# Attention and two feed-forward layers on one core: the values' products in float32, with each head's values among zeros

## The chip, the cores and the metric

The kernel runs on one core of a Trainium2 chip. The metric is the device time in microseconds, from the first instruction to the last, of one execution of the whole program. Three timed runs of the kernel before are given, and one execution with the hardware profiler, from which every row below is taken. The engines are called by the profile's short names: PE (TensorE's matrix products), PEld (its loads of the stationary operand), DVE (VectorE), ACT (ScalarE), POOL (GpSimd) and SP (SyncE, which here does nothing but issue DMAs).

## The reference, cut to what matters

Attention over 4 batches, 8 heads, 576 positions and a head size of 64, where each query sees itself and the 127 positions before it, with a penalty that grows with the distance; then a gated feed-forward layer of 1536 columns and a second one of 2048 columns over the 2304 rows that result. The weights come as float64.

```python
scores = scale * np.matmul(q, k.transpose(0, 1, 3, 2))
scores = np.where(mask, scores + bias[None], -1000000000.0)
attn = np.exp(scores - np.max(scores, axis=-1, keepdims=True))
attn = attn / (np.sum(attn, axis=-1, keepdims=True) + 1e-09)
x = np.matmul(attn, v)              # then heads side by side: 2304 x 512
x = (x @ w_a) * (x @ w_b) @ w_out   # 1536 columns between
h = x @ w_in
g = np.where(h >= 1, h, np.where(h <= -1, 0, (h + 1) ** 2 / 4))
out = g @ w_out2                    # 2048 columns between
```

## The kernel before, in words

**Two number formats on PE.** A float32 operand can be used as it is, and then the profile shows two matrix instructions and two weight loads for each product the program names (the scores of line 314 are named 144 times and stand in the profile 288 times). Or it is cut into a high and a low part of the type float32r, and three products are added: high by high, high by low, low by high. All feed-forward products do the latter (lines 576 to 578, 649, 677 to 679, 709 to 711); the parts are made by a copy that rounds (`ecopy`, or `nc.scalar.copy`) and a subtraction (`minus`, line 149).

**Attention** is cut into units: a batch, one of two parts of its positions (part 0 is positions 0 to 255, part 1 is 256 to 575), and a pair of heads. There are 32 units, taken batch by batch. A unit has rounds `m`, each for two blocks of 64 queries: `m` 0 and 1 in part 0, `m` 2, 3 and 4 in part 1, the last with one block alone. So there are 80 rounds, 20 in each batch. The two heads of a pair stand together in the 128 partitions: queries of head 0 in partitions 0 to 63, of head 1 in 64 to 127.

A round goes through three functions. `scores` (line 304) multiplies queries and keys (line 314), lets DVE add the penalty and find the maximum (line 320), ACT take the exponential with its sum (line 324), DVE add 1e-9 to the sum and invert it (lines 329 and 330), and then scales the first block's probabilities on POOL (line 338) and the second block's on ACT (line 334). `transposes` (line 343) turns the probabilities, three blocks of 128 columns in a full round, with a product by the identity matrix, and copies them from PSUM. `values` (line 396) multiplies them by the values, and every second round the sums go into the input of the feed-forward layer, high part by ACT and low part by DVE (lines 449 and 450), once for each head.

Values and probabilities are treated in two ways before. In batch 0 (the set `WHOLE`) they stay float32: a full round multiplies two whole blocks of 128 keys (lines 411 and 414), the first half of a block (64 rows, line 411) and a block `odd` whose first 64 rows are zero. In batches 1 to 3 they are cut in parts: POOL cuts the values (lines 292 and 293), ACT and DVE the turned probabilities (lines 389 and 391), which lie in tiles with zero quarters, and a full round is six float32r products of 256 columns (line 430), the round `m` = 0 three. The last round `m` = 4 is float32 everywhere, with a product of 128 rows and one of 64 (lines 407 and 408).

**Order of the work.** `attention` (line 461) is a generator of steps; for round `n` it emits the scores of `n`, the transposes of `n` - 3 and the values of `n` - 5. When a new unit begins it prepares the next unit (`prep_unit`) and issues the loads of the one after that (`load_unit`, `AHEAD` = 2). Between the products of the feed-forward layer the main loop takes steps of attention at a hand-set pace (`PACE`, 0.8 steps to a product group at first, then 0.5), and where products need rows that are not there (`ready`), it takes steps alone. The decoding of the float64 weights is emitted between them too (`pump`, `decode`): for the first 15 blocks two of its operations are POOL's (line 541 and the subtraction of line 543), the other five or six are DVE's. A scheduler then orders each engine's instructions by this order and by its own estimate of when each is ready; on the chip every engine takes its instructions strictly in that order. All DMAs are issued by SP, in one queue.

The first loads are `load_start` (line 201): queries, keys and values of batch 0, part 0, into tiles of the weights' pool (`wp`), whose first three slots they hold.

Of the kernel before, what the change touches and what calls it, by code (L numbers as in the profile page):

```python
# [26 lines left out]
def attention_and_two_ffns(  # L27
# [41 lines left out]
    E_V = ['PP', 'PP', 'PP', 'PP', 'PP', 'PP', 'PP', 'PP']  # L69
    E_VO = 'A'  # L70
    E_X = ['A', 'A', 'A', 'A', 'A', 'A', 'A', 'A']
    E_Y = 'AV'
    E_Z = 'P'
# [8 lines left out]
    NWHOLE = 2  # L82
# [3 lines left out]
    PW = 2  # L86
# [5 lines left out]
    VP = 2  # L92
    VT = 3
# [5 lines left out]
    WHOLE = {(0, p) for p in range(NWHOLE)}  # L99
# [26 lines left out]
    rel = att.tile([P, 2, 3 * D], F32, tag="s_sb", name="rel", bufs=SB)[:, 0]  # L126
# [57 lines left out]
    turned = []  # L184
    for z in range(PT):
        pair = tuple(
            att.tile([P, 4, P], F32R, tag=f"p{w}{z}", name=f"p{w}{z}", bufs=1) for w in "hl"
        )
        for t in pair:
            for me, at, other in ((slice(D), 1, slice(D, P)), (slice(D, P), 2, slice(D))):  # L190
                ecopy(
                    E_Z, t[me, at].rearrange("p (n t) -> p n t", t=D), diag[0][me, :2, other]
                )
        turned.append(pair)
# [6 lines left out]
    def load_start():  # L201
        for nm in "qkv":
            start[nm] = [
                wp.tile([P, H, D], F32, tag=f"w{z}", name=f"{nm}{z}") for z in "hl"
            ]
        src = {"q": q, "k": k, "v": v}
        for nm, h0, h1, hi_ in LORD:
            for t, t0 in zip(start[nm], (0, P)):
# [11 lines left out]
    def value_parts():  # L220
        return [att.tile([P, NV - 1, P], F32R, tag=f"v{z}", name=f"v{z}", bufs=VP) for z in "hl"]

    def turn_start(hp):
# [7 lines left out]
        for j in range(2):  # L231
# [3 lines left out]
        prep[0, 0, hp] = (  # L235
            qd, kt,
            [t[:, 2 * hp : 2 * hp + 2, :].rearrange("p h d -> p (h d)") for t in start["v"]],
            start["odd"][:, 2 * hp : 2 * hp + 2, :].rearrange("p h d -> p (h d)"),
        )

    def load_unit(b, part, hp):
# [15 lines left out]
        vt = att.tile([P, NV, 2, D], F32, tag="vt", name="vt", bufs=VT)  # L257
        n = (q1 - k0) // P
        for j in range(2):
            nc.sync.dma_start(  # L260
                vt[:, :n, j, :],
                v[b, 2 * hp + j, k0 : k0 + n * P, :].rearrange("(n p) d -> p n d", p=P),
            )
        if q1 == S:
            nc.sync.dma_start(
                vt[:D, n, :, :],
                v[b, 2 * hp : 2 * hp + 2, S - D :, :].rearrange("j p d -> p j d"),
            )
        prep[b, part, hp] = (t["q"], t["k"], vt)

    def prep_unit(u):
# [5 lines left out]
        qr, kr, vt = prep[b, part, hp]  # L277
# [8 lines left out]
        vt = vt.rearrange("p n j d -> p n (j d)")  # L286
        if (b, part) in WHOLE:
            prep[b, part, hp] = (qd, kt, vt, None)
            return
# [4 lines left out]
        prep[b, part, hp] = (qd, kt, vt, vs)  # L294
# [7 lines left out]
    rounds = {}  # L302

    def scores(b, hp, m):
        part = int(m >= 2)
        q0, _, k0 = PART[part]
        qd, kt = prep[b, part, hp][:2]
        ps = ps_at.tile([P, 2, 4 * D], F32, tag="at", name="ps_s")
        s_sb = att.tile([P, 2, 3 * D], F32, tag="s_sb", name="s_sb", bufs=SB)
# [8 lines left out]
        for z, i in enumerate(qblocks(m)):  # L318
            cs = slice(first_col(i), 3 * D)
            nc.vector.tensor_tensor_reduce(  # L320
                s_sb[:, z, cs], ps[:, z, cs], biases[hp][:, cs], -QSCALE, BIG,
# [3 lines left out]
                s_sb[:, z, cs], s_sb[:, z, cs], AF.Exp,  # L325
# [3 lines left out]
        nc.vector.tensor_scalar(ssum[:, :n], ssum[:, :n], 1e-9, None, ALU.add)  # L329
        nc.vector.reciprocal(ssum[:, :n], ssum[:, :n])  # L330
        for z, i in enumerate(qblocks(m)):
            cs = slice(first_col(i), 3 * D)
            if E_N[2 * b + part][z] == "A":
                nc.scalar.activation(
                    s_sb[:, z, cs], s_sb[:, z, cs], AF.Copy, scale=ssum[:, z : z + 1]
                )
                continue
            ENG[E_N[2 * b + part][z]].tensor_scalar(  # L338
                s_sb[:, z, cs], s_sb[:, z, cs], ssum[:, z : z + 1], None, ALU.mult
# [3 lines left out]
    def transposes(b, hp, m):  # L343


        s_sb = rounds.pop((b, hp, m)).rearrange("p z k -> p (z k)")
        ps = ps_at.tile([P, 4, P], F32, tag="at", name="ps_t")
        part = int(m >= 2)
        if (b, part) in WHOLE and m < ROUNDS - 1:
            if part and m == 2:  # L350
                vt = prep[b, part, hp][2]
                odd = start["odd"].rearrange("p (u n j) d -> p u n (j d)", u=2, n=2)[:, hp % 2]
                ecopy(E_VO, odd[D:], vt[D:, :2])
                prep[b, part, hp] = prep[b, part, hp][:3] + (odd,)
            pt = att.tile([P, 3, P], F32, tag="pt", name="pt", bufs=PW)
            for z in range(m == 0, 3):
                n = D if (m, z) == (0, 1) else P
                nc.tensor.transpose(ps[:n, z, :], s_sb[:, z * P : z * P + n], ident)
            if m == 0:
                ecopy(E_T[2 * b + (m >= 2)][0], pt[:D, 1], ps[:D, 1])  # L360
                ecopy(E_T[2 * b + (m >= 2)][1], pt[:, 2], ps[:, 2])
            else:
                ecopy(E_T[2 * b + (m >= 2)][0], pt, ps[:, :3])
            rounds[b, hp, m] = pt
            return
        if m == ROUNDS - 1:
            pt = att.tile([P, 3, P], F32, tag="pt", name="pt", bufs=PW)
            nc.tensor.transpose(ps[:, 0, :], s_sb[:, :P], ident)
            nc.tensor.transpose(ps[:D, 1, :], s_sb[:, P : P + D], ident)
            ecopy(E_T[2 * b + (m >= 2)][0], pt[:, 0], ps[:, 0])  # L370
            ecopy(E_T[2 * b + (m >= 2)][1], pt[:D, 1], ps[:D, 1])
            rounds[b, hp, m] = pt
            return
        count["t"] += 1
        ph, pl = turned[count["t"] % PT]
        if m == 0:
            nc.tensor.transpose(ps[:D, 1, :], s_sb[:, P : P + D], ident)
            nc.tensor.transpose(ps[:, 3, :], s_sb[:, 2 * P :], ident)
            cuts = [(slice(P), slice(3, 4), slice(3, 4)), (slice(D), slice(2, 3), slice(1, 2))]
        else:  # L380
            for z, at in enumerate((0, 1, 3)):
                nc.tensor.transpose(ps[:, at, :], s_sb[:, z * P : (z + 1) * P], ident)  # L382
            cuts = [
                (slice(P), slice(0, 4, 3), slice(0, 4, 3)),
                (slice(D), slice(2, 3), slice(1, 2)),
                (slice(D, P), slice(1, 2), slice(1, 2)),
            ]
        for n, (me, to, at) in enumerate(cuts):
            ecopy(E_T[2 * b + (m >= 2)][n > 0], ph[me, to], ps[me, at])
# [441 lines left out]
```

## Time and profile before

| | us |
|---|---|
| median of three runs | 1018.1 |
| the three runs | 1021.05, 1016.41, 1018.1 |
| the profiled execution's own time | 1016.69 |
| its span in the profile | 1014.9 |
| PE busy | 989.9 |
| DVE busy | 681.5 |
| ACT busy | 444.4 |
| POOL busy | 222.6 |

The span runs from the first to the last instruction that the profiler recorded; the execution's own time is 1.8 us longer. Busy times are unions of instruction spans. PE's instructions overlap in a pipeline and their ends are modelled, so PE can be busy without a break and still take its instructions at more than one pace: the distance from one start to the next tells more than the duration. An idle stretch in front of an instruction is put down to what ended it.

### The profile page before, as it was taken

Reading aid. Unit: us, or ns where it says so; the run is one execution under the profiler, and the core shown is the slowest. Engines: PE = TensorE matmul, PEld = TensorE weight load, DVE = VectorE, ACT = ScalarE, POOL = GpSimd, SP = SyncE. Lnnn points to the kernel's source line nnn. Section 1 sums busy time; section 2 is a strip of 40 time slices with the busy share of each in tenths; the row PEclk is TensorE's granted clock in tenths of the full one; section 3 lists DMA queues with packets and bytes.
Section 4 is the critical chain, followed back from the end, with each engine's and each line's share of the span. In section 5 each row is a group of like instructions: output and inputs, shape, how many; then the busy total and the mean of one; then the engine's idle time right before and its main releaser. Section 6 shows DMA issues by size and latency. Waiting matters only on the chain.

```text
span 1014.9 us, 15950 instructions
## 1 busy us (share of the span) xinstructions
PE 989.9 (98%) x5608; PEld 868.7 (86%) x5608; DVE 681.5 (67%) x1678; ACT 444.4 (44%) x1156; POOL 222.6 (22%) x268
## 2 busy tenths in 40 slices
PE   5899999999999999999999999999999999999998
PEld 4789899999999988888988888888888888888887
DVE  7998967868747899212898279833996446744443
ACT  5876677777644343111343234433552223322222
POOL 6685853544411100000122223000020000000001
PEclk9998999999999999999999999999999999999999
DMA  8756334335043443000223002200231000001111
GB/s 177 138 124 139 87 67 91 66 70 101 11 181 111 146 165 106 1 1 1 63 86 102 1 23 82 83 1 0 63 104 42 1 1 21 1 1 42 42 42 63
DMA packets 136512, 67.10 MB, mean 66 GB/s; under 512 B 107120, under 2 KB 127600, under 8 KB 135920
## 3 DMA queue, kind: packets, MB, share of 16 engines
q1 hardware_dynamic: 136432, 66.09, 24.4%
q8 instruction: 44, 0.72, 0.3%
q14 instruction: 36, 0.29, 0.1%
HBM read 56.62 MB, written 9.44 MB: 65 GB/s over the span
## 4 chain that ended last, share of the span: by engine, by line
PE 84%; DVE 3%; issue 1%; DMA 0%; ACT 0%; DVEq 0%; SPq 0%; ACTq 0%
PE mm L576 15%; PE mm L577 15%; PE mm L578 15%; PE acc L710 6%; PE acc L709 6%; PE acc L711 6%; PE acc L649 5%; PE acc L679 3%; PE acc L677 3%; PE acc L678 3%; PE ps_o L430 3%; PE ps_s L314 3%; PE ps_t L382 1%; PE ps_o L408 0%; DVE e L535 0%
## 5 line engine op out<-in xcount | busy, mean ns | idle before, releaser
L576 PE MATMUL mm<-xh,wh 128*128 128x512 f32 (+1 forms) x952 | 323.0, 340 | 1.9 <-DVE c_sb L633 0.8
L577 PE MATMUL mm<-xl,wh 128*128 128x512 f32 (+1 forms) x952 | 322.6, 339 | 0.8 <-DVE xl L149 0.8
L578 PE MATMUL mm<-xh,wl 128*128 128x512 f32 (+1 forms) x952 | 322.7, 339 | 0.0
L576 PEld LDWEIGHTS mm<-xh,wh 128*128 128x128 f32 x952 | 179.7, 189 | 22.9 <-DVE c_sb L633 1.2
L577 PEld LDWEIGHTS mm<-xl,wh 128*128 128x128 f32 x952 | 180.2, 189 | 20.8 <-DVE xl L149 1.1
L578 PEld LDWEIGHTS mm<-xh,wl 128*128 128x128 f32 x952 | 180.1, 189 | 19.4
L632 ACT ACTIVATE c_sb<-c_sb,half 128x512 f32<-128x512 f32 (+1 forms) x80 | 54.6, 682 | 166.6 <-DVE c_sb L631 166.6
L709 PE MATMUL acc<-wh,gh 128*128 128x512 f32 x288 | 112.3, 390 | 0.0
L710 PE MATMUL acc<-wl,gh 128*128 128x512 f32 x288 | 112.2, 390 | 0.0
L711 PE MATMUL acc<-wh,gl 128*128 128x512 f32 x288 | 110.4, 390 | 0.0
L631 DVE TENSOR_SCALAR c_sb<-mm 128x512 f32<-128x512 f32 (+1 forms) x80 | 50.8, 636 | 82.0 <-PE mm L578 79.2
L149 POOL TENSOR_TENSOR gl<-c_sb,gh 128x256 fp32r<-128x256 f32 x16 | 14.2, 891 | 386.3 <-ACT gh L598 379.2
L621 DVE TENSOR_TENSOR a_sb<-mm,a_sb 128x256 f32<-128x256 f32 (+1 forms) x79 | 40.7, 516 | 85.3 <-PE mm L578 77.3
L149 POOL TENSOR_TENSOR gl<-a_sb,gh 128x256 fp32r<-128x256 f32 x50 | 41.3, 827 | 236.2 <-ACT gh L598 236.2
L633 DVE SCALAR_TENSOR_TENSOR c_sb<-mm,c_sb 128x512 f32<-128x512 f32 (+1 forms) x80 | 50.7, 635 | 39.1 <-ACT c_sb L632 39.0
L338 POOL TENSOR_SCALAR s_sb<-s_sb,ssum 128x192 f32<-128x192 f32 (+1 forms) x80 | 62.5, 782 | 63.0 <-DVE ssum L330 39.0
L324 ACT ACTIVATE s_sb<-s_sb,nmax 128x192 f32<-128x192 f32 (+2 forms) x144 | 62.3, 434 | 25.7 <-DVE nmax L320 24.6
L598 ACT CAST gh<-c_sb 128x512 fp32r<-128x512 f32 (+1 forms) x80 | 46.3, 579 | 56.2 <-DVE c_sb L633 47.4
L598 ACT CAST gh<-a_sb 128x256 fp32r<-128x256 f32 (+1 forms) x79 | 38.2, 484 | 69.2 <-DVE a_sb L621 68.7
L525 ACT ACTIVATE e<-w 128x512 f32<-128x512 f32 x65 | 43.7, 673 | 56.6 <-DMA w<-in_moe_w_out_dram 11.8
L542 ACT CAST wh<-e 128x512 fp32r<-128x512 f32 x68 | 42.3, 621 | 59.3 <-DVE e L541 38.4
L149 DVE TENSOR_TENSOR gl<-c_sb,gh 128x512 fp32r<-128x512 f32 x64 | 44.2, 690 | 32.7 <-ACT gh L598 32.4
(112 smaller groups left out, 1891.4 us busy)
## 6 DMA issues: line engine op xcount, KB each, us to landing
w<-in_moe_w_out_dram SPq DMA_DIRECT2D x28, 512.0 KB, 3.5
w<-in_moe_w_in_dram SPq DMA_DIRECT2D x16, 512.0 KB, 3.6
w<-in_moe_w_a_dram SPq DMA_DIRECT2D x12, 512.0 KB, 4.3
w<-in_moe_w_b_dram SPq DMA_DIRECT2D x12, 512.0 KB, 4.5
x2p<-y SPq DMA_DIRECT2D x18, 256.0 KB, 2.2
out_dram<-osum SPq DMA_DIRECT2D x18, 256.0 KB, 2.0
xsum<-x2p SPq DMA_DIRECT2D x4, 1024.0 KB, 5.9
kraw<-in_k_dram SPq DMA_DIRECT2D x64, 56.0 KB, 2.7
```

Source lines behind the costliest of these rows:

```text
L149: eng.tensor_tensor(out_, a, hi.bitcast(F32), ALU.subtract)
L324: nc.scalar.activation(s_sb[:, z, cs], s_sb[:, z, cs], AF.Exp, bias=nmax[:, z : z + 1], scale=-1.0, accum_out=ssum[:, z : z + 1],)
L338: ENG[E_N[2 * b + part][z]].tensor_scalar(s_sb[:, z, cs], s_sb[:, z, cs], ssum[:, z : z + 1], None, ALU.mult)
L576: nc.tensor.matmul(ps, wh[:, cs], xh[:, c], start=(c == 0), stop=False)
L577: nc.tensor.matmul(ps, wh[:, cs], xl[:, c], start=False, stop=False)
L578: nc.tensor.matmul(ps, wl[:, cs], xh[:, c], start=False, stop=(c == NC - 1))
L598: nc.scalar.copy(hi[:, :n], t[:, :n])
L631: nc.vector.tensor_scalar(c_sb[:, :n], ph[:, :n], -1.0, None, ALU.max)
L632: nc.scalar.activation(c_sb[:, :n], c_sb[:, :n], AF.Square, bias=half, scale=0.5)
L709: nc.tensor.matmul(accs[s], gh[:, ss], wh, start=begin, stop=False)
L710: nc.tensor.matmul(accs[s], gh[:, ss], wl, start=False, stop=False)
L711: nc.tensor.matmul(accs[s], gl[:, ss], wh, start=False, stop=end)
```

## The change

The hi and lo parts of values and probabilities are gone in all batches, and so are `odd` and the products of 64 rows. Values are loaded into four standing tiles `vpad` of 4 blocks x 2 heads x 128 columns, where head 0's values fill columns 0 to 63 and head 1's columns 64 to 127, and POOL writes zeros into the other halves once. Probabilities are written into four standing tiles `padded` of 2 query blocks x 256 columns, the second block shifted by 64, with zeros around them. A round turns four blocks of 128 columns (two for `m` = 0 and `m` = 4) and copies them from PSUM at once. `values` multiplies, for each of two key blocks and each head, a 128 x 128 block of values among zeros by 128 columns of probabilities (64 in `m` = 4), in float32, all into the same 128 columns of PSUM; so both heads' sums lie under each other in the partitions, and go to the feed-forward input for both heads at once, after the last round of a part. The sum's 1e-9 is added on POOL and not on DVE, and POOL's scaling has a second factor of 1. Values are loaded when their unit begins and not two units ahead, each head's last 64 rows by a DMA of its own. The values of the start take four slots of `wp` in place of three for queries, keys and values, and eight DMAs in place of two.

```diff
-    turned = []
-    for z in range(PT):
...
+    padded = []
+    for z in range(SB):
+        t = att.tile([P, 2, 4 * D], F32, tag=f"s{z}", name=f"s{z}", bufs=1)
+        nc.gpsimd.memset(t[:, 0, 3 * D :], 0.0)
+        nc.gpsimd.memset(t[:, 1, :D], 0.0)
+        padded.append(t)
+    def clear_others(t):
+        for j in range(2):
+            nc.gpsimd.memset(t[:, :, j, (1 - j) * D : (2 - j) * D], 0.0)
+    vpad = []
+    for z in range(VT):
+        t = att.tile([P, NV, 2, P], F32, tag=f"v{z}", name=f"v{z}", bufs=1)
+        clear_others(t)
+        if TAIL < P:
+            nc.gpsimd.memset(t[TAIL:, NV - 1], 0.0)
...
+                for hp in range(NPAIR):
+                    for j in range(2):
+                        nc.sync.dma_start(
+                            start["v"][hp][:, :, j, j * D : (j + 1) * D],
+                            v[0, 2 * hp + j, : 2 * P, :].rearrange("(n p) d -> p n d", p=P),
+                        )
...
-        for _ in range(3):
+        for _ in range(4):
             slots[0][2].append(None)
-        odd = start["odd"] = att.tile([P, H, D], F32, tag="odd", name="odd", bufs=1)
-        nc.vector.memset(odd[:D], 0.0)
-        ecopy(E_VO, odd[D:], start["v"][0][D:])
...
+    def load_values(b, part, hp):
+        if b == 0 and part == 0:
+            return start["v"][hp]
...
+        vt = vpad[z]
         n = (q1 - k0) // P
         for j in range(2):
             nc.sync.dma_start(
-                vt[:, :n, j, :],
+                vt[:, :n, j, j * D : (j + 1) * D],
...
+            for j in range(2):
+                nc.sync.dma_start(
+                    vt[:TAIL, n, j, j * D : (j + 1) * D], v[b, 2 * hp + j, S - TAIL :, :]
+                )
...
-        vs = value_parts()
-        n = (q1 - k0) // P
-        ecopy(E_V[2 * b + part][0], vs[0][:, :n], vt[:, :n])
-        minus(ENG[E_V[2 * b + part][1]], vs[1][:, :n], vt[:, :n], vs[0][:, :n])
...
-        nc.vector.tensor_scalar(ssum[:, :n], ssum[:, :n], 1e-9, None, ALU.add)
+        nc.gpsimd.tensor_scalar(ssum[:, :n], ssum[:, :n], 1e-9, 1.0, ALU.add, ALU.mult)
         nc.vector.reciprocal(ssum[:, :n], ssum[:, :n])
...
+        for u in range(us.start, 2):
+            for z in range(n):
+                nc.tensor.transpose(ps[:, 2 * u + z, :], s_sb[:, z, u * P : (u + 1) * P], ident)
+        pt = att.tile([P, 2, 2, P], F32, tag="pt", name="pt", bufs=PT)
+        ecopy(
+            E_T[2 * b + part][0], pt[:, us, :n], ps.rearrange("p (u z) t -> p u z t", z=2)[:, us, :n]
+        )
...
+        opens, closes = m in (0, 2), m in (1, ROUNDS - 1)
...
+        todo_ = [(u, j) for u in range(m == 0, 2) for j in range(2)]
+        for e, (u, j) in enumerate(todo_):
+            nc.tensor.matmul(
+                dst, vt[:, m - 1 + u - k0 // P, j, :], pt[:, u, :n, j * D : (j + 1) * D],
+                start=opens and e == 0, stop=e == len(todo_) - 1, skip_group_check=True,
+            )
...
-            for j in range(2):
-                me = slice(j * D, (j + 1) * D)
...
-                ecopy(E_X[2 * b + part], xh, src)
-                minus(nc.vector, xl, src, xh)
+            xh, xl = (x[:, hp, t - t0 : t - t0 + w] for x in xs[i])
+            ecopy(E_X[2 * b + part], xh, po[:, at : at + w])
+            minus(nc.vector, xl, po[:, at : at + w], xh)
...
+                    values_of[units[u]] = load_values(*units[u])
```

## Rows read from the trace of the kernel before

**Rows 1.** The page's head and its busy times by engine.

```profile
span 1014.9 us, 15950 instructions
PE 989.9 (98%) x5608; PEld 868.7 (86%) x5608; DVE 681.5 (67%) x1678; ACT 444.4 (44%) x1156; POOL 222.6 (22%) x268
```

**Rows 2.** Busy time by stretch, with instructions; then granted clock, DMA share, GB/s.

```profile
0.00:33.00 33.00, 19.80 (x96) 15.99 (x97) 27.30 (x98) 20.23 (x67) 19.93 (x37) 0.95 0.82 172
33.00:85.00 52.00, 46.74 (x299) 40.57 (x298) 47.06 (x157) 39.54 (x129) 38.36 (x38) 0.93 0.58 127
100.00:125.00 25.00, 23.56 (x182) 22.39 (x181) 24.46 (x77) 16.97 (x57) 20.66 (x21) 1.00 0.44 100
150.00:200.00 50.00, 50.00 (x403) 49.23 (x401) 40.79 (x173) 37.91 (x143) 23.17 (x35) 1.00 0.40 77
```

**Rows 3.** Who waited for whom before 85 us, DVE's waits, the two longest.

```profile
DVE e L527 <- DMA w<-in_moe_w_a_dram: 3.2, 1, 3.2
DVE s_sb L320 <- PE ps_s L314: 3.0, 2, 2.7
```

**Rows 4.** PE's timeline near 204 us: start, duration, line, shape, count.

```profile
204.13 0.81 PE L314 MATMUL ps_s<-kt,diag 128*128 128x192 f32 x4
204.78 0.49 PE L382 MATMUL ps_t<-ident,s_sb 128*128 128x128 f32 x3
...
205.22 0.29 PE L430 MATMUL ps_o<-pl,vh 128*128 128x256 f32 x1
205.34 0.28 PE L430 MATMUL ps_o<-ph,vl 128*128 128x256 f32 x1
```

**Rows 5.** PE's timeline: a round `m` = 0 from 91.66, its scores.

```profile
91.66 0.61 PE L314 MATMUL ps_s<-kt,diag 128*128 128x64 f32 x4
...
92.22 0.28 PE L576 MATMUL mm<-xh,wh 128*128 128x256 f32 x1
```

**Rows 6.** PE's timeline: values of a last round, and of full rounds of batch 0.

```profile
141.26 0.38 PE L407 MATMUL ps_o<-pt,vt 128*128 128x128 f32 x2
...
142.21 0.28 PE L649 MATMUL acc<-gh,wl 128*128 128x256 f32 x1
...
45.78 1.13 PE L416 MATMUL ps_o<-pt,vt 64*128 64x128 f32 x6 [0.63 <-ACT pt L155]
...
47.06 1.13 PE L416 MATMUL ps_o<-pt,vt 64*128 64x128 f32 x6
```

**Rows 7.** Groups of instructions with shapes: count, busy us, mean ns, idle before.

```profile
L149 DVE TENSOR_TENSOR xl<-ps_o,xh 64x256 fp32r<-64x256 f32 x40 | 16.8, 419 | 3.2 <-ACT xh L155 2.2
L329 DVE TENSOR_SCALAR ssum<-ssum 128x2 f32<-128x2 f32 x64 | 14.4, 227 | 4.7 <-ACT s_sb L324 4.4
L338 POOL TENSOR_SCALAR s_sb<-s_sb,ssum 128x192 f32<-128x192 f32 x64 | 53.6, 839 | 51.3 <-DVE ssum L330 30.2 <-PE ps_s L314 5.8 <-ACT xh L155 4.3
L338 POOL TENSOR_SCALAR s_sb<-s_sb,ssum 128x64 f32<-128x64 f32 x16 | 8.9, 555 | 11.7 <-DVE ssum L330 8.8 <-PE ps_o L416 1.3 <-DMA w<-in_moe_w_b_dram 1.0
masks.py:197 POOL MEMSET ident<- 128x128 f32 x1 | 0.2, 206 | 0.3 <-POOLq L815 0.3
```

**Rows 8.** DVE's and POOL's timelines: one DVE line beside two kinds of POOL work.

```profile
32.38 1.30 DVE L528 TENSOR_SCALAR e<-e 128x512 f32<-128x512 f32 x1
32.13 1.27 POOL L541 TENSOR_TENSOR e<-up,e 128x512 f32<-128x512 f32 x1 [1.98 <-DVE ssum L330]
40.86 0.43 DVE L528 TENSOR_SCALAR e<-e 128x512 f32<-128x512 f32 x1
40.82 1.02 POOL L338 TENSOR_SCALAR s_sb<-s_sb,ssum 128x192 f32<-128x192 f32 x1 [0.99 <-DVE ssum L330]
```

**Rows 9.** SP's queue: a load of the start, and its longest wait on values.

```profile
12.17 0.47 SPq L210 DMA_DIRECT2D vh<-in_v_dram  x1
SPq L260 <- PE ps_o L408: 22.3, 5, 20.0
```

**Rows 10.** Busy time by stretch, as in group 2, from 77 to 84 us.

```profile
77.00:84.00 7.00, 6.91 (x26) 6.24 (x27) 4.18 (x21) 3.57 (x14) 4.74 (x6) 0.51 0.70 150
```

More of the change, by code (lines that the diff above doesn't have):

```diff
@@ L98, in attention_and_two_ffns @@
     WP = 15
-    WHOLE = {(0, p) for p in range(NWHOLE)}
     HP = lambda n: n < HPN
@@ L181, in attention_and_two_ffns @@
         diag.append(t)
-    turned = []
-    for z in range(PT):
[L186 to L194, printed above, removed]
+    padded = []
[13 more added lines that the diff above has]
+            nc.gpsimd.memset(t[TAIL:, NV - 1], 0.0)
+        vpad.append(t)
     prep = {}
@@ L201, in load_start @@
     def load_start():
-        for nm in "qkv":
+        for nm in "qk":
             start[nm] = [
@@ L205, in load_start @@
             ]
+        start["v"] = [
+            wp.tile([P, 2, 2, P], F32, tag=f"w{z}", name=f"v{n}{z}") for n in range(2) for z in "hl"
+        ]
+        for t in start["v"]:
+            clear_others(t)
         src = {"q": q, "k": k, "v": v}
         for nm, h0, h1, hi_ in LORD:
+            if nm == "v":
+                for hp in range(NPAIR):
[4 more added lines that the diff above has]
+                        )
+                continue
             for t, t0 in zip(start[nm], (0, P)):
@@ L234, in turn_start @@
         ecopy(E_S[2], kt[:, : 2 * P].rearrange("p (a t) -> p a t", t=P), ps[:, 2:4, :])
[L235 to L239, printed above, removed]
+        prep[0, 0, hp] = (qd, kt)
     def load_unit(b, part, hp):
@@ L256, in load_unit @@
             t[nm] = raw.rearrange("p n d -> p (n d)")[:, : q1 - s0]
-        vt = att.tile([P, NV, 2, D], F32, tag="vt", name="vt", bufs=VT)
+        prep[b, part, hp] = (t["q"], t["k"])
+    held = {}
+    def load_values(b, part, hp):
+        if b == 0 and part == 0:
+            return start["v"][hp]
+        _, q1, k0 = PART[part]
+        z = units.index((b, part, hp)) % VT
+        assert all(r in done for r in held.get(z, ()))
+        held[z] = [r for u, r in todo if units[u] == (b, part, hp)]
+        vt = vpad[z]
         n = (q1 - k0) // P
@@ L276, in prep_unit @@
         q0, q1, k0 = PART[part]
-        qr, kr, vt = prep[b, part, hp]
+        qr, kr = prep[b, part, hp]
         qd = diag[u % NDIAG]
@@ L306, in scores @@
         q0, _, k0 = PART[part]
-        qd, kt = prep[b, part, hp][:2]
+        qd, kt = prep[b, part, hp]
         ps = ps_at.tile([P, 2, 4 * D], F32, tag="at", name="ps_s")
-        s_sb = att.tile([P, 2, 3 * D], F32, tag="s_sb", name="s_sb", bufs=SB)
+        count["t"] += 1
+        s_sb = padded[count["t"] % SB]
+        at = lambda z, i: s_sb[:, z, first_col(i) + z * D : 3 * D + z * D]
         nmax = att.tile([P, 2], F32, tag="nmax", name="nmax", bufs=6)
@@ L343, in transposes @@
     def transposes(b, hp, m):
-        s_sb = rounds.pop((b, hp, m)).rearrange("p z k -> p (z k)")
+        s_sb = rounds.pop((b, hp, m))
         ps = ps_at.tile([P, 4, P], F32, tag="at", name="ps_t")
         part = int(m >= 2)
[L349 to L387, printed above, removed]
@@ L394, in attention_and_two_ffns @@
+        ecopy(
+            E_T[2 * b + part][0], pt[:, us, :n], ps.rearrange("p (u z) t -> p u z t", z=2)[:, us, :n]
+        )
+        rounds[b, hp, m] = pt
     outs = {}
@@ L434, in values @@
-        if m % 2 == 0 and m < ROUNDS - 1:
+        n = len(qblocks(m))
+        c = 2 * m * D - q0
+        dst = po[:, c : c + n * D].rearrange("p (n t) -> p n t", t=D)
+        todo_ = [(u, j) for u in range(m == 0, 2) for j in range(2)]
[4 more added lines that the diff above has]
+            )
@@ L435, in values @@
+        if not closes:
             return
-        t, end = b * S + 4 * (m // 2) * D, b * S + min(S, 2 * (m + 1) * D)
+        t, end = b * S + q0, b * S + q1
         at = 0
@@ L486, in ready @@
         return all(
-            t in done for _, t in todo if t[0] * S + 4 * (t[2] // 2) * D < t1
+            t in done for _, t in todo if t[0] * S + PART[int(t[2] >= 2)][0] < t1
         )
```

85 lines of the change are left out of this document (15 added, 70 removed).

## The prediction

> **What bounds the kernel now.** I read four views in this order: the page's busy times, the same by stretch, PE's timeline for the distance between starts, and who waited for whom. The page says that PE is busy for 989.9 of 1014.9 us [rows 1]; that is too coarse, for the stretches show two regimes. From 150 us on PE has no break, with 403 instructions in 50 us at full clock, while DVE has 9 us in 50 to spare [rows 2]. There, time is PE's instructions multiplied by their distances, and nothing else. Before 85 us, where batch 0 is worked on, PE's rows have gaps, and DVE is busy for 27.3 of 33 and 47.1 of 52 us [rows 2]; its waits there are two longer ones, 3.2 and 3.0 us, both in the first 14 us [rows 3]. So DVE, which decodes weights, sets the pace of the head. Between the two, from 85 to 150 us, batch 1 begins: 182 instructions in 25 us against 201 in the same time later [rows 2], so PE still starves for some 19 x 0.12 = 2.3 us.
>
> Prices on PE come from starts. Float32r products of 256 columns start 0.12 us apart [rows 4]. Three transposes and one such product take 205.22 - 204.78 = 0.44 us, so a transpose costs (0.44 - 0.12) / 3 = 0.107. Four float32 passes of 192 columns take 0.65 [rows 4], that is 0.162 each, and by columns 0.108 for 128. Two passes of 64 and two of 128 columns together with one product of 0.12 take 0.56 [rows 5]: 0.56 - 0.12 - 0.22 = 0.22 for the two short ones, so a pass of 64 columns costs 0.11 as well. A float32 product is two passes, 0.22 us.
>
> **The change part by part.**
>
> *PE, batches 1 to 3.* A full round had 6 x 0.12 = 0.72 for values and 3 x 0.107 = 0.32 for transposes, 1.04 together; it gets 4 products of two passes, 8 x 0.11 = 0.88, and 4 x 0.107 = 0.43, 1.31 together: +0.27. There are 3 batches x 4 pairs x 3 = 36 of these: +9.7. The round `m` = 0 goes from 0.36 + 0.21 to 0.44 + 0.21: +0.08 x 12 = +1.0. In the last round, two float32 products took 142.21 - 141.26 - 0.12 = 0.83 [rows 6], where four passes are worth 0.44; the 0.39 above that is what going to 64 rows and back costs. Now there are eight passes, 0.88: +0.05 x 12 = +0.6. Sum **+11.3 us**, nearly all where PE has no break, so on the path.
>
> *PE, batch 0.* A full round takes 47.06 - 45.78 = 1.28 [rows 6]; eight passes without the change of rows are 0.88, and a fourth transpose is added: -0.29 x 12 = -3.5; the four rounds `m` = 0 lose one change of rows each, -0.4 x 4 = -1.6. These 5 us lie beside DVE, which is the slower one there [rows 2, 3], so I count nothing.
>
> *DVE in the head.* Sums leave for both heads at once: 8 subtractions of 256 columns fewer at 0.42 [rows 7], and 4 short ones: -4. Twenty additions of 1e-9 go, 0.23 each by their mean [rows 7]; but this mean holds stretches in which DVE stood still for POOL and that will fall on the next instruction, so I take half: -2. DVE is released of 6 us; the ends are 0 and -9.
>
> *The addition on POOL.* New is a wait: the reciprocal, still on DVE, now follows POOL's addition, and behind the waiting reciprocal everything on DVE queues, the next round's maximum (for which ACT's exponential waits), the decoding, the low parts. No row shows POOL at two columns. Its scaling takes 0.84 at 192 and 0.56 at 64 columns [rows 7], so by the line through both some 0.42 at none (an estimate). Lower end of the wait: none, where the scheduler puts other DVE work between, as it does now between exponential and reciprocal; upper end: 0.42 and half of a 1.27 us decoding step ahead in POOL's queue [rows 8], 1.05 a round, 21 us in 20 rounds. I take 0.1 a round, +2, nearest to the row of today's waits, since DVE in the head runs late and finds its inputs ready [rows 3]. Head: -6 + 2 = **-4**, ends -9 and +15. In batches 1 to 3 the same wait costs nothing while DVE has 9 us in 50 spare [rows 2] and loses its subtractions of probabilities. If that cover were gone, 60 rounds at 0.1 would be 6 us.
>
> Here a rule speaks against the change. Beside a two-input step of POOL a one-input DVE instruction took 1.30 us, and beside POOL's scaling, begun just before, the same line took 0.43 [rows 8]: only the first kind holds DVE up. The Trainium skill, "SBUF — State Buffer", section "SBUF: two separate sides", says that DVE in its two-port mode and any GpSimd instruction exclude each other for the whole instruction. By the page each new addition would hold DVE; the scaling row differs, and I go by it.
>
> *85 to 300 us.* Starving there, 2.3 us by the count above in one stretch and less in others, should shrink as DVE is freed: **-4** for 85 to 300 in all, ends 0 and -8.
>
> *POOL and ACT.* POOL loses the cutting of values and twelve copies at the start, and gets 28 small clearings, by the one of 128 columns at 0.21 us [rows 7] some 6 us. POOL is busy 19.9 of the first 33 us [rows 2] and has room for them; only if they push its first decoding steps back do they cost, up to 3. ACT gets one longer copy for two or three short ones and half of the copies to the input; it is busy 39.5 of 52 us [rows 2] and no bound. Cost nothing.
>
> *SP.* Six more loads at the start, 0.5 each [rows 9], push the first loads of part 1 back by 3 us; batch 0's first maxima are not among them, and the wait on DVE may be 1. Sixteen more small loads later lie in a queue that has slack. That values load when their unit begins leaves five rounds before they are needed; today's loads wait for a buffer up to 20 us [rows 9], and with four tiles that wait goes, which frees the queries and keys queued behind it. Cost nothing; the cover is the five rounds.
>
> *The rest.* The pace and the order of steps stay; after 300 us nothing changes. Holding sums of part 1 one round longer needs one more round before `ready`, which the pace has ahead.
>
> **Sum.** Against the profiled execution's own 1016.7: +11.3 - 4 - 4 = +3.3, so 1020. The median shown is 1.4 above that execution: **1021.5**.
>
> **The rivals.**
>
> *POOL's addition holds the head (slower).* Place: DVE, 10 to 85 us. For it: POOL is busy 38.4 of 52 us there [rows 2] with steps of 1.3, and DVE and POOL then wait for each other in each round. Against it: DVE's present row of waits. From 0.3 us a round on it eats the 6 us released; at 0.8 it costs 16 - 6 = +10 in place of -4: 1021.5 + 14 = 1035.5.
>
> *The head gives back more (faster).* DVE is released of 9 with no wait, all starving of 8 goes, and PE's clock does not fall: the granted clock was 0.51 on the mean from 77 to 84 us [rows 10], mostly the 1.2 GHz level, so some 3 us of delay. For it: DVE bounds the head, and batch 0's PE work shrinks. Then -9 - 8 - 3 + 11.3 = -8.7: 1009.5 with the 1.4. Against it: POOL's longer chain.
>
> *Passes come cheaper.* Were a pass of 64 columns worth half, the twelve last rounds would save 0.44 each, and 4 in batch 0 unseen: 1021.5 - 5 = 1016.5. Against it: [rows 5]. The Trainium skill, "TensorE: Matmul & The Clock Gate", section "Back-to-back issue gap", gives some 81 ns for a product of 128 columns with its weight load; by the page eight passes would be 0.65, under the 0.72 of today, and the time some 1004. The rows say 0.11, and I go by them.
>
> **How the numbers follow.** Forecast 0.45, POOL's addition 0.25, the head 0.23, cheaper passes 0.07. A measurement of this kernel tells 0.5%, 5.1 us, from no change: the bounds are 1013 and 1023.2. The forecast, 1016 to 1027, splits into 0.29 same and 0.16 slower; the first rival 0.21 slower, 0.04 same; the second 0.19 faster, 0.04 same; the third 0.03 faster, 0.04 same. That is faster 0.22, same 0.41, slower 0.37. The range must reach into both rivals: 1007, somewhat below the second, to 1036, just above the first; the upper end of the wait, 1041, is left out.
>
> **What would show it.** In the profile after: values' passes 0.11 apart, eight to a round, and no extra 0.4 in last rounds; PE without a break from 100 us on; attention's last subtraction some 7 us later than before counted from 85 us. The forecast is wrong if DVE shows waits of its reciprocal on POOL of over 6 us in the head, if PE's 50-us stretches after 150 us still have gaps, or if attention ends earlier than before.

## The result and the profile after

The kernel after takes 1023.75 us (median of four runs, 1023.48 to 1023.99), the kernel before 1017.58 beside it: a ratio of 1.0055, with the interval 1.003 to 1.008. It is slower by about half a per cent. Run beside the experiments below, the kernel before has higher medians, 1018.9 to 1020.0, so the 6.2 us between these two medians may be 2 us too much. The forecast was 1021.5 with a range from 1007 to 1036: the measured time lies inside it and 2.2 us above the forecast. The sum's own value, 1020 for the profiled execution, has to be held against that execution's own 1023.88: it was 4 us too low.

The page's head of the kernel after answers to [rows 1]: DVE has 57 us less to do, POOL 34 us less, PE 6 us more, and the span is 7 us longer.

```profile
span 1022.0 us, 15819 instructions
PE 995.5 (97%) x5804; PEld 883.1 (86%) x5804; DVE 624.0 (61%) x1393; ACT 411.5 (40%) x975; POOL 188.2 (18%) x316
```

Busy times by stretch, with the columns of [rows 2], which they answer to:

```profile
0.00:33.00 33.00, 19.48 (x95) 16.34 (x96) 26.68 (x84) 18.39 (x60) 24.89 (x62) 0.90 0.72 164
33.00:85.00 52.00, 46.30 (x361) 43.67 (x360) 49.41 (x142) 37.20 (x116) 36.68 (x51) 1.00 0.67 145
85.00:100.00 15.00, 13.74 (x110) 13.33 (x110) 14.61 (x45) 11.32 (x37) 10.60 (x15) 1.00 0.72 149
100.00:125.00 25.00, 23.89 (x198) 23.65 (x198) 16.35 (x62) 17.96 (x59) 12.97 (x26) 1.00 0.46 92
125.00:150.00 25.00, 25.00 (x211) 24.98 (x211) 10.93 (x50) 14.12 (x48) 5.39 (x16) 1.00 0.33 69
150.00:200.00 50.00, 50.00 (x418) 50.00 (x417) 22.02 (x91) 28.75 (x93) 13.10 (x34) 1.00 0.37 73
```

Two stretches of the kernel before that [rows 2] leave out:

```profile
85.00:100.00 15.00, 15.00 (x119) 14.50 (x119) 14.27 (x55) 11.94 (x45) 8.62 (x10) 1.00 0.63 130
125.00:150.00 25.00, 25.00 (x198) 24.36 (x197) 17.17 (x78) 18.67 (x71) 13.86 (x19) 1.00 0.31 67
```

From 150 us on PE has no break in either kernel, so I take that stretch as each kernel's full pace, an estimate, since the mixture of instructions is not the same everywhere. At 403 instructions in 50 us the kernel before would have started 524 between 85 and 150 us and started 119 + 182 + 198 = 499: 25 too few, 3.1 us of starving. After, at 418 in 50 us, 543 would have started and 519 did: 24 too few, 2.9 us. By this count the starving is the same; PE's idle time in the rows, from 85 to 150 us, is 1.4 us before and 2.4 after, so it did not shrink either. Before, nearly all of it lay from 100 to 125 us; after, it lies from 85 to 125 us, more than half of it before 100 us, where DVE is busy for 14.61 of 15 us.

What was done by 85 us shows in PE's groups from 0 to 85 us (instructions, busy us, mean ns, idle before). Before:

```profile
L576 PE MATMUL mm<-xh,wh 128*128 128x256 f32 x24 | 7.0, 317 | 0.7 <-ACT wh L542 0.4 <-ACT a_sb L616 0.3
...
L408 PE MATMUL ps_o<-pt,vt 64*128 64x128 f32 x6 | 1.5, 322 | 0.0
```

After:

```profile
L385 PE MATMUL ps_o<-pt,v 128*128 128x128 f32 (+1 forms) x96 | 13.4, 271 | 0.0
...
L526 PE MATMUL mm<-xh,wh 128*128 128x256 f32 x33 | 10.0, 323 | 0.0
```

With their sister lines (24 + 24 + 24 and three times 12 before, 33 + 33 + 31 and three times 12 after) that is 108 feed-forward products before and 133 after: 25 more, 25 x 0.12 = 3.0 us ahead. Attention is ahead as well, by about one round: before, the fourth last round of batch 0 is still to come (lines 407 and 408 have 6 of 8 passes each), while after all of the batch's 4 x 36 = 144 values' passes are done (96 + 48). So the head gave 3 to 5 us, and what came behind it took 11 again: attention's last subtraction of a low part starts at 298.9 us, before at 295.7, and from there on each feed-forward product starts 7 us later than the same product before, to the end.

PE's timeline after, with the columns of [rows 4]: transposes and values of a full round, then a last round (64 columns):

```profile
201.17 0.60 PE L361 MATMUL ps_t<-ident,s 128*128 128x128 f32 x4
201.52 0.36 PE L599 MATMUL acc<-gh,wh 128*128 128x256 f32 x1
201.72 0.28 PE L599 MATMUL acc<-gl,wh 128*128 128x256 f32 x1
...
202.32 1.05 PE L385 MATMUL ps_o<-pt,v 128*128 128x128 f32 x8
203.13 0.36 PE L599 MATMUL acc<-gh,wh 128*128 128x256 f32 x1
203.33 0.28 PE L599 MATMUL acc<-gl,wh 128*128 128x256 f32 x1
...
153.16 1.00 PE L385 MATMUL ps_o<-pt,v 128*128 128x64 f32 x8
153.97 0.36 PE L526 MATMUL mm<-xh,wh 128*128 128x256 f32 x1
154.18 0.28 PE L527 MATMUL mm<-xl,wh 128*128 128x256 f32 x1
```

Four transposes and one product take 201.72 - 201.17 = 0.55, so the transposes 0.43. Eight passes of 128 columns take 203.33 - 202.32 - 0.12 = 0.89, eight of 64 columns 154.18 - 153.16 - 0.12 = 0.90. The forecast had 0.43, 0.88 and 0.88.

The granted clock is a second difference in the head. Before, it was 0.51 from 77 to 84 us [rows 10], near the 1.2 GHz level (PE had been busy for 14.5 of the 17 us before it), and DVE then had the longer of its two waits for PE's scores:

```profile
83.02 0.36 DVE L320 CUSTOM_DVE_ANT_0 s_sb<-ps_s,bias 128x192 f32<-128x192 f32 x1 [2.70 <-PE ps_s L314]
```

After, the same stretch has the full clock, 45 instructions on PE for 26, and DVE's longest wait for scores in the head is 1.4 us:

```profile
77.00:84.00 7.00, 5.81 (x45) 5.27 (x44) 6.85 (x21) 4.01 (x14) 4.05 (x6) 1.00 0.74 154
```

The start shows a difference that the forecast did not have. SP's queue and PE's first rows, before:

```profile
0.72 0.43 SPq L210 DMA_DIRECT2D qh<-in_q_dram  x1
...
2.93 0.45 PE L229 MATMUL ps_q<-ident,qh 128*128 128x128 f32 x1 [2.93 <-DMA qh<-in_q_dram]
```

And after:

```profile
0.74 0.44 SPq L462 DMA_DIRECT2D w<-in_moe_w_a_dram  x1
1.24 0.49 SPq L462 DMA_DIRECT2D w<-in_moe_w_b_dram  x1
1.77 1.01 SPq L218 DMA_DIRECT2D v0h<-in_v_dram  x2
2.83 0.98 SPq L218 DMA_DIRECT2D v0l<-in_v_dram  x2
3.85 0.47 SPq L225 DMA_DIRECT2D qh<-in_q_dram  x1
...
7.87 0.80 PE L237 MATMUL ps_q<-ident,qh 128*128 128x128 f32 x2 [7.87 <-DMA qh<-in_q_dram]
```

Two weight blocks and four loads of values now stand ahead of the first queries, which are issued 3.1 us later, and PE begins 4.9 us later.

DVE's waits after (us in total, times, longest), the three next to the longest before 85 us, which answer to [rows 3]; then one from 85 to 310 us:

```profile
DVE e L478 <- ACT e L475: 1.5, 1, 1.5
DVE s L331 <- PE ps_s L325: 1.4, 1, 1.4
DVE up L482 <- POOL e L491: 1.4, 2, 1.1
...
DVE ssum L341 <- POOL ssum L340: 21.0, 26, 1.7
```

The wait of the reciprocal (line 341) on POOL's addition (line 340), the slower rival's place, is not among DVE's waits in the head (the longest one left out above is 2.5 us for the first weights). Later it is 21 us, where DVE has more than half of its time to spare.

POOL's groups after (columns of [rows 7]): the scaling, 839 and 555 ns before, and the new addition, estimated at 0.42 us. Up to 90 us both are slower than in these means of the whole, 586 ns for the scaling at 192 columns (969 before) and 297 for the addition:

```profile
L346 POOL TENSOR_SCALAR s<-s,ssum 128x192 f32<-128x192 f32 x64 | 30.4, 476 | 32.0 <-DVE ssum L341 24.5 <-PE ps_o L385 4.2 <-PE ps_t L361 1.8
L340 POOL TENSOR_SCALAR ssum<-ssum 128x2 f32<-128x2 f32 x64 | 15.5, 243 | 92.8 <-ACT s L335 91.2
L346 POOL TENSOR_SCALAR s<-s,ssum 128x64 f32<-128x64 f32 x16 | 6.1, 379 | 4.8 <-DVE ssum L341 4.8
```

### The profile page after: what moved, and what is told of

The parts are those of the page before. It is cut to its first block, busy times and chain, and to the rows that moved or that the text cites. A ratio compares the mean times of both kernels' runs of the same rounds, so it can differ in the third digit from the quotient of the medians.

```text
span 1022.0 us, 15819 instructions
## 1 busy us (share of the span) xinstructions
PE 995.5 (97%) x5804; PEld 883.1 (86%) x5804; DVE 624.0 (61%) x1393; ACT 411.5 (40%) x975; POOL 188.2 (18%) x316
## 4 chain that ended last, share of the span: by engine, by line
PE 86%; DVE 2%; DMA 1%; issue 0%; POOL 0%; ACT 0%; DVEq 0%; POOLq 0%; SPq 0%; ACTq 0%
PE mm L526 15%; PE mm L527 15%; PE mm L528 15%; PE acc L661 6%; PE acc L660 6%; PE acc L659 6%; PE acc L599 5%; PE ps_o L385 4%; PE ps_s L325 3%; PE acc L627 3%; PE acc L628 3%; PE acc L629 3%; PE ps_t L361 2%; DMA w<-in_moe_w_out_dram 1%; DVE e L485 0%
## 5 line engine op out<-in xcount | busy, mean ns | idle before, releaser
L526 PE MATMUL mm<-xh,wh 128*128 128x512 f32 (+1 forms) x952 | 332.1, 349 | 0.0
L335 ACT ACTIVATE s<-s,nmax 128x192 f32<-128x192 f32 (+2 forms) x144 | 62.1, 432 | 55.0 <-DVE nmax L331 54.4
L385 PE MATMUL ps_o<-pt,v 128*128 128x128 f32 (+1 forms) x528 | 71.4, 273 | 1.9 <-DVE nmax L331 1.1
L331 DVE CUSTOM_DVE_ANT_0 s<-ps_s,bias 128x192 f32<-128x192 f32 (+2 forms) x144 | 42.9, 329 | 48.9 <-PE ps_s L325 48.8
L385 PEld LDWEIGHTS ps_o<-pt,v 128*128 128x128 f32 x528 | 66.1, 191 | 2.5 <-DVE nmax L331 1.3
```

The lines of the kernel that those rows point to most:

```text
L335: nc.scalar.activation(at(z, i), at(z, i), AF.Exp, bias=nmax[:, z : z + 1], scale=-1.0, accum_out=ssum[:, z : z + 1],)
L385: nc.tensor.matmul(dst, vt[:, m - 1 + u - k0 // P, j, :], pt[:, u, :n, j * D : (j + 1) * D], start=opens and e == 0, stop=e == len(todo_) ...
L526: nc.tensor.matmul(ps, wh[:, cs], xh[:, c], start=(c == 0), stop=False)
```

## The experiments

All times are medians of 5 to 12 runs; the kernel before, run beside them, had medians of 1018.9 to 1020.0 in 17 to 30 runs. The kernel after was not run again beside them; its variant with one factor, below, was, and took 1023.66.

### What the products and transposes on PE cost

**One product less** (in the kernel after):

```diff
+        if b >= 2 and m in (1, 2, 3):
+            todo_ = todo_[:3]
```

> The changed kernel with the fourth of the four products of values left out in the full rounds of batches 2 and 3, 24 products of two passes. Theory (from 100 us on time is PE's passes, 0.22 us to a product): 24 x 0.22 = 5.3 us less, 1018 to 1019. Rival (another engine's chain sets that stretch): 1022 to 1024. The output of those batches lacks that part of the sums.

Measured 1018.79 (1018.30 to 1019.37), 5.0 less than after, 0.21 us to a product. The price of 0.22 us holds, and all of it is on the path.

**Each transpose twice** (in the kernel after):

```diff
-                nc.tensor.transpose(ps[:, 2 * u + z, :], s_sb[:, z, u * P : (u + 1) * P], ident)
+                for _ in range(2 if b >= 2 and m in (1, 2, 3) else 1):
+                    nc.tensor.transpose(ps[:, 2 * u + z, :], s_sb[:, z, u * P : (u + 1) * P], ident)
```

> The kernel after, but in the full rounds of batches 2 and 3 each transpose is done twice into the same place (24 rounds, 4 transposes more in each); nothing is left out. Theory: where PE has no break a transpose costs its 0.107 us whatever stands beside it, so 24 x 4 x 0.107 = +10.3 us against the kernel after (1023.75): about 1034, and attention's last product some 10 us later. Rival: transposes slip in beside the float32 products' weight loads, so that the fourth transpose of the change cost half or nothing and the +0.27 of a full round was the products' alone: +5 or less, under 1029.

Measured 1034.68 (1034.11 to 1035.06): +10.9, and attention's last subtraction starts at 309.1 us, 10.2 later. The rival falls: a transpose costs its 0.107 to 0.114 us in full.

**Last rounds of 128 rows, in the kernel before:**

```diff
-            nc.tensor.transpose(ps[:D, 1, :], s_sb[:, P : P + D], ident)
-            ecopy(E_T[2 * b + (m >= 2)][0], pt[:, 0], ps[:, 0])
-            ecopy(E_T[2 * b + (m >= 2)][1], pt[:D, 1], ps[:D, 1])
+            nc.tensor.transpose(ps[:, 1, :], s_sb[:, P : 2 * P], ident)
+            ecopy(E_T[2 * b + (m >= 2)][0], pt[:, :2], ps[:, :2])
...
-            nc.tensor.matmul(po[:, 0, :], vt[:D, at, :], pt[:D, 1], start=False, stop=True)
+            nc.tensor.matmul(po[:, 0, :], vt[:, at, :], pt[:, 1], start=False, stop=True)
```

(and two clearings of the rows and columns that are new).

> The kernel before with the last round of each unit of part 1 in products of 128 rows alone: POOL clears the second block's upper rows, and the 64-row product, transpose and copies become 128-row ones. Theory (going to 64 rows and back costs PE 0.39 us, and PE is the path after 85 us): 12 rounds x 0.39 = 4.7 us less, 1013 to 1015. Rival (the 0.39 is a modelled end and no time): 1017 to 1019.

Measured 1013.82 (1011.52 to 1016.74), ratio 0.9958 with the interval 0.9939 to 0.9976: faster than both kernels. PE's timeline of a last round in this kernel:

```profile
140.56 0.38 PE L409 MATMUL ps_o<-pt,vt 128*128 128x128 f32 x2
140.78 0.39 PE L410 MATMUL ps_o<-pt,vt 128*128 128x128 f32 x2
140.92 0.36 PE L651 MATMUL acc<-gl,wh 128*128 128x256 f32 x1
141.12 0.28 PE L651 MATMUL acc<-gh,wl 128*128 128x256 f32 x1
```

The two float32 products take 141.12 - 140.56 - 0.12 = 0.44 in place of 0.83 in [rows 6]: 0.39 us is what going to 64 rows and back cost. The 5.1 us are against the median of the kernel before beside this run, 1018.9; the two profiled executions, 1013.20 and 1016.69, are only 3.5 apart. The edit also makes one copy of two in each last round, which was not tried by itself. In the kernel after, the last rounds did without the change of rows too, but paid it back with twice as many passes.

### What the first loads cost

**The start's values in the standing tiles** (in the kernel after; they then hold two slots fewer of the weights' pool, and the queries and keys go first again):

```diff
-        start["v"] = [
-            wp.tile([P, 2, 2, P], F32, tag=f"w{z}", name=f"v{n}{z}") for n in range(2) for z in "hl"
-        ]
-        for t in start["v"]:
-            clear_others(t)
+        start["v"] = vpad
...
-                            start["v"][hp][:, :, j, j * D : (j + 1) * D],
+                            start["v"][hp][:, :2, j, j * D : (j + 1) * D],
...
-        for _ in range(4):
+        for _ in range(2):
```

> The changed kernel with the start's values loaded into the four standing value tiles in place of four slots of the weights' pool, so that queries and keys stand first in SP's queue again (they came 5 us later after the change). Theory (the late queries cost the first rounds 1.6 to 4.9 us and the head never gets them back): 1019 to 1022. Rival (DVE sets the head whatever comes first): 1023 to 1024.5.

Measured 1019.77 (1018.51 to 1022.21), 4.0 less than after and within the measurement of the kernel before (1.0012, 0.9999 to 1.0025). PE's first row in it:

```profile
2.85 0.45 PE L233 MATMUL ps_q<-ident,qh 128*128 128x128 f32 x1 [2.85 <-DMA qh<-in_q_dram]
```

So the start is worth 4 us, though DVE and not PE is the busier engine in the head: DVE's part of every round begins with scores, and the first of those came 1.6 us later after the change than before (12.8 us for 11.2; 11.0 in this run). The edit also frees two slots of the weights' pool and drops eight of POOL's clearings. The slots brought no weights sooner at first: the fourth to sixth weight blocks are loaded at 17.1, 23.2 and 30.8 us in the kernel after and at 18.1, 23.7 and 33.1 here. The clearings were not tried by themselves, so that the order of the loads is the cause is likely and not shown alone.

### DVE and POOL in the head

**The addition of 1e-9 back on DVE** (in the kernel after):

```diff
-        nc.gpsimd.tensor_scalar(ssum[:, :n], ssum[:, :n], 1e-9, 1.0, ALU.add, ALU.mult)
+        nc.vector.tensor_scalar(ssum[:, :n], ssum[:, :n], 1e-9, None, ALU.add)
```

> The changed kernel (1023.75 us) with one part undone: 1e-9 is added to the sums on DVE again, as before. Theory (the 36 + 12 + 12 longer rounds of batches 1 to 3 on PE, +11.3 us, decide, and the addition on POOL costs the head little): 1022 to 1026, and DVE in the first 85 us is busy some 2 us more. Rival (the reciprocal's wait on POOL holds the head): 1015 to 1020.

Measured 1025.82 (1024.47 to 1027.58): 2 more, not 4 to 9 less. POOL's addition does not hold the head; moving it there gained 2 us. Up to 85 us DVE is busy for 79.6 us with the addition and for 76.1 without.

**POOL's scaling without the second factor** (in the kernel after):

```diff
-                at(z, i), at(z, i), ssum[:, z : z + 1], 1.0, ALU.mult, ALU.mult
+                at(z, i), at(z, i), ssum[:, z : z + 1], None, ALU.mult
```

> The changed kernel with POOL's scaling of the probabilities in its old form, one factor and no second factor of 1. If the second factor is what took this instruction from 839 to 476 ns at 192 columns, its mean goes back to about 840 ns. Theory (in the head DVE and POOL get in each other's way, so POOL's time counts there, and after 100 us nothing but PE counts): 20 rounds of the head with up to 0.36 us each, 1024 to 1030. Rival (POOL's time is beside the path everywhere): 1023 to 1024.5.

Measured 1023.66 (1023.25 to 1023.97), no change, with the scaling back at 841 ns:

```profile
L346 POOL TENSOR_SCALAR s<-s,ssum 128x192 f32<-128x192 f32 x64 | 53.8, 841 | 28.6 <-DVE ssum L341 25.2 <-PE ps_o L385 2.0 <-ACT gh L548 0.4
```

So 23 us of POOL's time are beside the path here.

**One of POOL's two decoding steps on DVE** (in the kernel with the early queries; each of the first 15 weight blocks has a word in the list `DEC`, whose last letter places the low part's subtraction):

```diff
-'VVPP'
-'AVPP'
+'VVPV'
+'AVPV'
```

> The changed kernel with the start's order mended (1019.8 us), and of the first 15 weight blocks the subtraction of the low part on DVE, not POOL: 15 x 0.70 = 10.5 us more for DVE, 15 x 1.42 = 21 us of two-input work less for POOL. Theory (DVE is held up by POOL's two-input steps, so the head is set by the two together): what DVE gains in waits pays for what it gets, 1017 to 1023. Rival (DVE alone sets the head): 1026 to 1031.

Measured 1020.66 (1018.13 to 1021.24): +0.9 for 10.5 us more work on DVE, less than either kernel's runs spread.

**Both steps on DVE** (the words become `VVVV` and `AVVV`):

> The kernel after with the start's loads in the order queries, keys, values (1019.77), and for the first 15 weight blocks both two-input decoding steps moved from POOL to DVE: 30 steps of some 0.70 us, 21 us more work for DVE before 90 us, none of these steps on POOL. Theory: beside POOL's two-input steps DVE's one-input steps stretch from 0.43 to as much as 1.3 us, so DVE gets much of the 21 us back by running its own steps at 0.4 to 0.45: 1018 to 1027, and the means of the decoding steps fall below 0.5 and 0.75. Rival: POOL's steps run beside DVE at no cost to it and DVE alone sets the head: 21 us more DVE work end 21 us later, some 1038.

Measured 1022.19 (1020.33 to 1023.09): +2.4 for 21 us more work. DVE's decoding groups from 0 to 90 us, in the kernel with the early queries:

```profile
L479 DVE TENSOR_SCALAR e<-up 128x512 uint32<-128x512 uint32 x13 | 9.1, 697 | 0.1
L474 DVE TENSOR_SCALAR e<-e 128x512 f32<-128x512 f32 x14 | 8.5, 608 | 0.8 <-ACT e L471 0.7
```

And with both steps on DVE:

```profile
L474 DVE TENSOR_SCALAR e<-e 128x512 f32<-128x512 f32 x11 | 4.6, 421 | 1.1 <-ACT e L471 1.0
L479 DVE TENSOR_SCALAR e<-up 128x512 uint32<-128x512 uint32 x10 | 4.3, 430 | 0.0
```

The same steps fall from 697 and 608 to 430 and 421 ns once POOL has no two-input decoding steps, though POOL still scales and adds. (With one of the two moved, the first of them fell to 416 and the second stayed, at 639.) DVE's busy time in all, with thirty steps more than in the kernel with the early queries, is 622.7 us for 619.5. So POOL's two-input steps cost DVE nearly what they take off it; it is the two engines together that set the pace of the head.

### The faster scaling in the kernel before: not settled

**The second factor alone**, in the kernel before:

```diff
-                s_sb[:, z, cs], s_sb[:, z, cs], ssum[:, z : z + 1], None, ALU.mult
+                s_sb[:, z, cs], s_sb[:, z, cs], ssum[:, z : z + 1], 1.0, ALU.mult, ALU.mult
```

> The kernel before with the second factor of 1 in POOL's scaling and nothing else. Its mean at 192 columns should fall from 839 to about 480 ns, some 29 us of POOL in all. Theory (after the run with one factor showed no change: POOL's time is beside the path): the same within 0.3%, 1016 to 1020. Rival (before, POOL had the cutting of values too and its time counts): 1012 to 1016.

Measured 1020.61 (1019.50 to 1025.20), ratio 1.0029 (1.0015 to 1.0044): a little slower, which neither the theory nor the rival expected.

**Both, last rounds of 128 rows and the second factor:**

> The kernel before with both, the second factor and the last rounds of 128 rows. If they add: the run with 128 rows alone, within 2 us; if POOL's shorter scaling makes room for its clearings in the head: 1 to 3 us under it.

Measured 1018.79 (1017.35 to 1020.27): 5 more than without the factor, so the two do not add. From about 20 us on the scheduler orders the instructions otherwise, and POOL waits once 4.9 us for DVE's addition to a sum (line 332). The clock at the start is not what it lost by: the granted clock was 1.00 for the first 33 us. From 125 to 150 us PE started 184 instructions, with the single factor 204. Why is open.

**The second factor in batches 1 to 3 alone**, with last rounds of 128 rows:

> The kernel before with last rounds of 128 rows (1013.82), and POOL's scaling with a second factor of 1 in batches 1 to 3 alone; batch 0 keeps the single factor. With the factor in all batches it was 1018.79. Theory: the 5 us are lost in the head, where another order of the instructions lets POOL wait 4.9 us for one reciprocal and PE's clock fall, and later POOL's time is beside the path: 1012 to 1015.5, and the first 85 us as with the single factor. Rival: a faster POOL costs wherever it runs, since its steps then fall on DVE's at other moments: three of four batches' worth, 1017.5 or more.

Measured 1019.38 (1012.73 to 1022.76). The kernel before beside it had 1019.99, 1.1 more than beside the run with 128 rows alone, so about 1 of the 5.6 us may not be the kernel's. The time is the rival's, but the trace does not show its mechanism. Stretches with the columns of [rows 2], for the single factor:

```profile
20.00:25.00 5.00, 4.09 (x22) 3.05 (x21) 4.62 (x19) 4.91 (x18) 4.67 (x5) 0.78 0.89 187
25.00:33.00 8.00, 6.15 (x39) 4.73 (x39) 7.86 (x32) 6.80 (x26) 4.85 (x6) 1.00 0.82 158
```

And for this kernel:

```profile
20.00:25.00 5.00, 4.42 (x17) 3.28 (x16) 4.20 (x19) 4.92 (x18) 4.32 (x5) 0.50 0.83 187
25.00:33.00 8.00, 7.37 (x29) 6.04 (x30) 5.44 (x24) 5.39 (x21) 3.83 (x5) 0.61 0.85 162
```

Up to 33 us both have the same instructions in the same order on every engine, for batch 0 has the single factor in both. Yet here the granted clock was 0.50 and 0.61, at or near the 1.2 GHz level, and PE started 46 instructions in 13 us, not 61. In the 20 us before, PE had been busy for 8.2 us here and for 9.1 there. Over the twelve executions the span mostly goes with the mean granted clock: 1020.7 and 1021.0 at 0.984, 1013.3 and 1013.5 at 0.994, 1011.0 at 0.997; but one at 0.995 took 1016.8. What lets the clock fall in one execution and not in another, with the same order of work, stays open, and so does whether the faster scaling has any part in it.

**Last rounds of 128 rows, and the low part's subtraction on DVE**, in the kernel before:

> The kernel before with last rounds of 128 rows (1013.82), and for the first 15 weight blocks the low part's subtraction moved from POOL to DVE: 15 x 0.70 = 10.5 us more work for DVE. Theory, from the same move in the kernel after, which cost 0.9 us: 1012 to 1017, no gain or loss to be measured. Rival: in the kernel before DVE has more work in the head (681 us in all against 624), so the move costs most of its 10 us: 1020 or more.

Measured 1014.36 (1012.25 to 1016.59): no different from 1013.82. Both beat the two kernels, and the moved step adds nothing to the last rounds of 128 rows.

## Why the prediction was right in its number, and where its steps were wrong

| step | forecast | in the runs |
|---|---|---|
| PE, batches 1 to 3 | +11.3 | about +11 by the prices after (passes 0.89 a round, transposes 0.43, row change 0.39; a product left out and transposes doubled cost what they should) |
| head | -4 | -3 to -5 by what was done at 85 us |
| starving, 85 to 300 us | -4 | 0 by the count (3.1 us before, 2.9 after) |
| profiled execution to median | +1.4 | -0.1 |

With the third row at nothing the sum is +7.3, and the profiled executions differ by 1023.88 - 1016.69 = 7.2. **The step that failed is "85 to 300 us: -4".** It took for granted that a DVE with less to do ends the starving. The starving shrank where it stood, from 100 to 125 us (198 instructions for 182), and came back earlier, from 85 to 100 us (110 for 119). The place is shown; why is argued: PE came to batch 1 sooner, while DVE was still decoding there. DVE and POOL did finish sooner (the low part of the fifteenth weight block is done at 110 us, before at 129), but not before PE needed them.

That the median came out only 2.2 above the forecast is luck, for the last step failed the other way. The kernel after repeats itself within 0.5 us, while the executions of the kernel before spread over 4.6; the one profiled was near their lower end.

**The head's -4 was right by misses that cancel.** "SP: cost nothing" was wrong: it looked at the first loads of part 1 and not at where the new loads and the weights' loads fall against the first queries; that is +4, by the run that puts the queries first again. So without the late start the head would have given some 8, near the forecast's own end of -9. Of DVE's release, the additions were worth 2 as forecast, and the wait on POOL's addition, put at +2, is not there: the addition takes 0.243 us in the mean and 0.297 in the head, not 0.42, and the row of waits in the head does not name it. The rival with 1035.5 falls with that.

The third miss is the clock. The forecast read both of DVE's longer waits in the head as lying in the first 14 us; the longer wait for PE's scores, 2.70 us, ends at 83.02 us, in the stretch with the clock at 0.51. After, the low clock there and the wait are gone, as the faster rival had it ("some 3 us"). With DVE's release at 6 us as forecast, no wait on POOL, +4 for the start and -2.7 for this, the head comes to -4.7. (From 0 to 33 us the clock was lower after, 0.90 for 0.95. That cost little: the run with one product less took 1018.30 in an execution with 1.00 there and 1018.79 in the median.) The -4.7 is a sum from two traces: no run changes the clock alone, and the 4 us put for the fewer subtractions were not tried.

What the release did not buy shows in the decoding. From 0 to 90 us four of the five decoding steps that are always DVE's took 28 us for 46 before, 0.61 each, and 40 us for 52 after, 0.78 each. Of the pages weighed in the forecast, "SBUF — State Buffer" of the Trainium skill, section "SBUF: two separate sides", has one engine block the other for a whole instruction. The kernel with no two-input decoding steps on POOL agrees with that for these steps (608 to 421 ns), and not for POOL's scaling and addition, beside which DVE's steps ran at 421.

**The rival of cheaper passes falls** on its own row: passes of 64 columns cost what those of 128 do (0.90 and 0.89 for eight). The 81 ns that the Trainium skill's "TensorE: Matmul & The Clock Gate", section "Back-to-back issue gap", led to are not what the trace shows for a float32 pass, 0.11 us. (The 1004 that the forecast drew from them holds only with transposes at 81 ns as well; with the passes alone its sum gives some 1009.) The faster rival's head of -9 was nearly there, but with the 4 us of the late start on top and no starving gone. Of the forecast's signs, passes 0.11 apart, no extra 0.4 in last rounds and an end of attention later by some 7 us counted from 85 us came true (3.2 us later, from a head 3 to 5 us ahead); PE without a break from 100 us on did not, it is idle for 1.1 us up to 125.

That POOL's 28 clearings, ACT and the values' later loads cost nothing is in accord with the times: no wait on the clearings or the values' loads stands among DVE's in the head, and on ACT one of 1.5 us. They were not tried by themselves.

## What to carry to other kernels

Price a change of number format by the distance from start to start, transposes, short products and changes of row count included: here a full round with float32 products and zeros came out some 0.27 us dearer than with cut ones, 0.16 of it the products and 0.11 a fourth transpose, while the cheapest gain was to stop changing to 64 rows. When loads are added at the start, write down the queue's order anew and look at what stands ahead of the first operand. And time freed on an engine is worth nothing until the trace shows what takes its place: here it went into steps that two engines hold up for each other, and into the same starving 15 us sooner.

## What was not expected of the hardware

- A second factor of 1 in POOL's scaling shortens it, from 839 to 476 ns at 192 columns and from 555 to 379 at 64. It changed the time of the kernel after by nothing.
- Going from 128 rows to 64 and back costs PE 0.39 us a round, nearly as much as two float32 products.
- From 20 to 25 us the granted clock was 0.50 in the profiled execution of one kernel and 0.78 in that of another, with the same instructions in the same order up to there. The executions of the first spread over 10 us, the longer ones mostly with the lower mean clock.
